# The last token chunk transposed by one DMA, into a tile-major layout

## The chip, the cores and the metric

One core of a Trainium2 chip. The metric is the device time of one execution, in microseconds (us). A profile is one execution taken by the hardware profiler; its times count from the start of its span. Engines: TensorE (PE, with weight loads apart as PEld), VectorE (DVE), ScalarE (ACT), GpSimd (POOL), and SyncE (SP), which here only issues DMAs. L12 is line 12 of the kernel.

## The reference

Tokens x are 2048 x 512, in bf16. They are normalised, and two branches are added to x: a filter in the frequency domain over both axes, and a gated MLP of width 1792.

```python
x = A_x                                   # (1, 2048, 512)
xn = _layernorm(x, axis=-1)
# A: rfft2 over tokens and features, times w_r + 1j * w_i (2048 x 257), irfft2
# B: h = gelu(xn @ w_gate) * (xn @ w_up);  h @ w_down
return x + _A_ref(xn, A_w_r, A_w_i) + _B_ref(xn, B_w_gate, B_w_up, B_w_down)
```

## The kernel before, in words

**Tiling.** The tokens are 16 tiles of 128 (j), and these are four chunks of 512 (m for the filter, b for the MLP). x stays in SBUF as `x_sb` with tokens on the partitions. Both branches contract over features, so both need the normalised tokens transposed: `xnT` (L251), features on 128 partitions, four groups of 128 features (dc), 2048 tokens in a row for each group, in fp16.

**How a chunk gets into xnT.** `ln_stat` and `ln_aggr` (L379 to L389) make mean and variance on DVE, and the reciprocal deviation on POOL. `ln_norm` (L391) writes one normalised tile into `xn`, a ring of four tiles, 128 x 2048 in all, which shares the buffer `cmx` with `ev1`. `trans` (L395) has TensorE transpose eight 128x128 blocks into a PSUM bank (L402), and then one copy puts the bank into `xnT`: DVE for feature groups 0 and 1 (L412), ACT for 2 and 3 (L414). A chunk takes two calls. Chunk 0 is done in part tile by tile by `trans1` (L1005 to L1014).

**Who reads xnT.** `butter` (L416) adds and subtracts feature halves on DVE: L422 and L423 over two feature groups of a chunk (1024 elements a partition each), L425 and L426 after them over 512. The results, the folds, are the stationary operands of `unit_D` (L430, matmuls L439 to L443), one call a tile, the first step of the filter's transform. From there `units_A` stores to DRAM (scr1, on SP), `load_tv` reads back (on SP), and `unit_B` (L571), `unit_C` and, near the end, `unit_E` and `unit_F` follow. `gate` and `up` (L859, L873) read xnT as the moving operand, 512 tokens at a time, in four matmuls over the feature groups (L868, L883); ACT makes the gelu (L871), DVE the product hT (L889). `product` (L743) is the down projection, done in seven products over sums (`sum_01`, L705; `sums_S`, L687; `sums_T`, L734) in place of eight. The sums are written over parts of xnT that are no longer read: `sum_01` over chunk 0's place, `sums_S` for the last chunk over that of chunks 0 to 2.

**What sets the order.** `_Prog.op` appends each operation to the list of its engine in program order, and derives the semaphore waits from keys read and written; each engine runs its list in order. The main loop (b, then the 14 feature groups fc) emits gate and up. After each of them `hook` runs the calls that were planned for that hook's number with `at(h, ...)`. Chunk 3's normalisation is planned at hooks 23 to 29, its two trans at 33 and 34, butter(3) at 35 and 36, unit_D(12) to (15) at 39 to 42, units_A(3) at 44, load_tv(3) at 47. On SP, the loads of filter weights `load_W` (L340) for slot 1 are planned at hooks 29 and 30, and load_tv(1) at 30, in this order. PSUM banks are chosen by `take` (L324), which keeps an estimate of when each bank comes free; each call moves the estimates of all later ones.

```python
            at(t, (trans, m, (0, 1), (0, 1, 2, 3)))
            at(t + 1, (trans, m, (2, 3), (0, 1, 2, 3), "act"))
            at(t + 2, (butter, m, 0))
            at(t + 3, (butter, m, 1))
```

Of the kernel before, what the change touches and what calls it, by code (L numbers as in the profile page):

```python
# [8 lines left out]
ALU = mybir.AluOpType  # L9
BF16 = mybir.dt.bfloat16  # L10
F16 = mybir.dt.float16
F32 = mybir.dt.float32  # L12

S = 2048
# [4 lines left out]
P = 128  # L19
NJ = 16  # L20
# [194 lines left out]
def bass_parallel_sum__spectral_gfnet__glu_gated_geglu__prompt_kernel(  # L215
# [27 lines left out]
    with ExitStack() as es:  # L243
        def sb(name, shape, dt):
            return es.enter_context(nc.sbuf_tensor(name, shape, dt))

        pr = _Prog(nc, es)
        op = pr.op

        x_sb = sb("x_sb", [P, NJ, D], BF16)  # L250
        xnT = sb("xnT", [P, 4, S], F16)  # L251
        arena = sb("arena", [P, 8192], F16)
        am = arena[:, 0:3072].rearrange("p (j c) -> p j c", j=NJ)
        fold = [arena[:, 4096 + 2048 * i:6144 + 2048 * i].rearrange("p (a c) -> p a c", a=4) for i in range(2)]
# [2 lines left out]
        wg_sb = sb("wg", [P, 4, FF], BF16)  # L257
        wu_sb = sb("wu", [P, 4, FF], BF16)
# [10 lines left out]
        ev1 = cmx[:, 0:1024].rearrange("p (a c) -> p a c", a=2)  # L269
        xn = cmx[:, 1024:3072].rearrange("p (a d) -> p a d", a=4)  # L270
# [23 lines left out]
        row = sb("row", [32, 64], BF16)  # L294
# [16 lines left out]
        def bank(i):  # L311
            return psum[:, i * 512:(i + 1) * 512]

        def bank_h(i):
            return psum_h[:, i * 1024:(i + 1) * 1024]
# [79 lines left out]
        def trans(m, dcs, jjs, eng="dve"):  # L395
            bk = take(1, 0.45, 1.2)
            def f(e):
                ins = None
                for a, dc in enumerate(dcs):
                    for c, jj in enumerate(jjs):  # L400
                        i = a * len(jjs) + c
                        ins = e.transpose(bank_h(bk)[:, i * P:(i + 1) * P], xn[:, jj, dc * P:(dc + 1) * P], ident[:])  # L402
                return ins
            op("pe", f, r=["ident"] + [("xn", jj) for jj in jjs], w=[("ps", bk)])
            w = len(jjs) * P
            c0 = m * 512 + jjs[0] * P
            n = len(dcs)
            dst = xnT[:, dcs[0]:dcs[0] + n, c0:c0 + w]
            src = bank_h(bk)[:, 0:n * w].rearrange("p (a c) -> p a c", a=n)
            ks = [("xnT", m, dc, jj) for dc in dcs for jj in jjs]  # L410
            if eng == "dve":
                op("dve", lambda e: e.tensor_copy(dst, src), r=[("ps", bk)], w=ks)  # L412
            else:
                op("act", lambda e: e.activation(dst, src, ACT.Copy), r=[("ps", bk)], w=ks)  # L414

        def butter(m, part):  # L416
            f = fold[m % 2]
            k = ("fold", m % 2)
            sl = slice(m * 512, (m + 1) * 512)
            xk = [("xnT", m, dc, jj) for dc in range(4) for jj in range(4)]  # L420
            if part == 0:
                op("dve", lambda e: e.tensor_tensor(ev1, xnT[:, 0:2, sl], xnT[:, 2:4, sl], ALU.add), r=xk, w=["ev1"])  # L422
                op("dve", lambda e: e.tensor_tensor(f[:, 2:4, :], xnT[:, 0:2, sl], xnT[:, 2:4, sl], ALU.subtract), r=xk, w=[k + (2,), k + (3,)])  # L423
            else:
                op("dve", lambda e: e.tensor_tensor(f[:, 0, :], ev1[:, 0, :], ev1[:, 1, :], ALU.add), r=["ev1"], w=[k + (0,)])  # L425
                op("dve", lambda e: e.tensor_tensor(f[:, 1, :], ev1[:, 0, :], ev1[:, 1, :], ALU.subtract), r=["ev1"], w=[k + (1,)])  # L426
# [225 lines left out]
               r=r + keys + [("x", j, 0), ("x", j, 1)], w=keys)  # L652

        eb7 = [early[:, 1792 * k:1792 * k + 1792].rearrange("p (f c) -> p f c", f=7) for k in range(4)]
        xb = xnT[:].rearrange("p d s -> p (d s)")
        cb = cmx[:]

        def ssum(b, k, f0, f1):
            if b == 2:
                return eb7[k][:, f0:f1, :]  # L660
            if k == 3:
                v = cb[:, 256 * f0:256 * f1]
            elif f1 <= 6:
                v = xb[:, 2048 * k + 256 * f0:2048 * k + 256 * f1]
            else:
                v = xb[:, 2048 * 3 + 256 * k:2048 * 3 + 256 * k + 256]
            return v.rearrange("p (f c) -> p f c", c=256)

        def s_keys(b, k, f0, f1):
# [45 lines left out]
        def s01(b, p, k, f0, f1):  # L715
            q = b == 0 and p == 1
            if k == 0 and b + p == 0:
                v = twh[:, 1024 + P * f0:1024 + P * f1]
            elif k == 0:
                v = arena[:, 7168 + P * f0:7168 + P * f1]  # L720
            else:
                assert f1 <= 4 or f0 >= 4
                o = P * (f0 % 4)
                if q and k in (1, 3):
                    v = fd[:, o:o + P * (f1 - f0)] if f0 >= 4 else dumm[:, o:o + P * (f1 - f0)]
                else:
                    row = 2 * (k == 2) + (f0 >= 4)
                    v = xb[:, 2048 * row + o:2048 * row + o + P * (f1 - f0)]
            return v.rearrange("p (f c) -> p f c", c=P)

        def sums_T(k):
# [127 lines left out]
        def gate(b, fc, jjs=(0, 1, 2, 3)):  # L859
            k = gun[0]  # L860
            n = len(jjs) * P
            c0 = b * 512 + jjs[0] * P
            bg = take(1, 0.0017 * n)

            def fn(e):
                ins = None
                for dc in range(4):
                    ins = e.matmul(bank(bg)[:, 0:n], wg_sb[:, dc, fc * P:(fc + 1) * P], xnT[:, dc, c0:c0 + n], start=(dc == 0), stop=(dc == 3))  # L868
                return ins
            op("pe", fn, r=[("wg", fc)] + [("xnT", b, dc, jj) for dc in range(4) for jj in jjs], w=[("ps", bg)])  # L870
            op("act", lambda e: e.activation(gl[k % 3][:, 0:n], bank(bg)[:, 0:n], ACT.Gelu_apprx_tanh), r=[("ps", bg)], w=[("gl", k % 3)])  # L871

        def up(b, fc, jjs=(0, 1, 2, 3), wait=False):  # L873
            k = gun[0]
            gun[0] += 1
            n = len(jjs) * P
            c0 = b * 512 + jjs[0] * P
            bu = take(1, 0.0017 * n, 2.2)

            def fn(e):  # L880
                ins = None
                for dc in range(4):
                    ins = e.matmul(bank(bu)[:, 0:n], wu_sb[:, dc, fc * P:(fc + 1) * P], xnT[:, dc, c0:c0 + n], start=(dc == 0), stop=(dc == 3))  # L883
                return ins
            op("pe", fn, r=[("wu", fc)] + [("xnT", b, dc, jj) for dc in range(4) for jj in jjs], w=[("ps", bu)])
            h0 = jjs[0] * P

            def mult():
                op("dve", lambda e: e.tensor_tensor(hT[b % 2][:, fc, h0:h0 + n], bank(bu)[:, 0:n], gl[k % 3][:, 0:n], ALU.mult),  # L889
                   r=[("ps", bu), ("gl", k % 3)], w=[("hT", b % 2, fc, jj) for jj in jjs])  # L890
            if wait:
                later.append(mult)
            else:
                mult()
# [28 lines left out]
        def at(h, *calls):  # L923
            plan.setdefault(int(h), []).extend(calls)
# [12 lines left out]
        for i in range(4):  # L937
            f0, f1 = (0, 4, 8, 11, 14)[i:i + 2]
# [12 lines left out]
        for m in range(1, 4):  # L951
            a = (5, 15, 23)[m - 1]
            t = (16, 25, 33)[m - 1]
            for i in range(4):
                at(a + i, (ln_stat, 4 * m + i))
            at(a + 3, (ln_aggr, 4 * m, 4))
            for i in range(4):
                at(a + 5 + i // 2, (ln_norm, 4 * m + i))
            at(t, (trans, m, (0, 1), (0, 1, 2, 3)))
            at(t + 1, (trans, m, (2, 3), (0, 1, 2, 3), "act"))  # L960
            at(t + 2, (butter, m, 0))
            at(t + 3, (butter, m, 1))
        at(3, (butter, 0, 0))
# [35 lines left out]
        def trans1(j, engs):  # L999
            for i, eng in enumerate(engs):  # L1000
                bk = take(1, 0.12, 1.0)
                def f(e, i=i, bk=bk):
                    ins = None
                    for a in range(2):
                        ins = e.transpose(bank_h(bk)[:, a * P:(a + 1) * P], xn[:, j, (2 * i + a) * P:(2 * i + a + 1) * P], ident[:])  # L1005
                    return ins
                op("pe", f, r=["ident", ("xn", j)], w=[("ps", bk)])
                dst = xnT[:, 2 * i:2 * i + 2, j * P:(j + 1) * P]
                src = bank_h(bk)[:, 0:256].rearrange("p (a c) -> p a c", a=2)
                ks = [("xnT", 0, 2 * i + a, j) for a in range(2)]  # L1010
                if eng == "dve":
                    op("dve", lambda e, dst=dst, src=src: e.tensor_copy(dst, src), r=[("ps", bk)], w=ks)
                else:
                    op("act", lambda e, dst=dst, src=src: e.activation(dst, src, ACT.Copy), r=[("ps", bk)], w=ks)  # L1014
# [108 lines left out]
```

## Time and profile before

| | |
|---|---|
| median of 13 runs | 183.08 us (182.71 to 184.56) |
| the profiled execution | 183.06 us, span 181.2 us |
| busy: PE, DVE, ACT, POOL | 175.1, 133.6, 95.7, 54.5 us |
| DMA | 26.84 MB, mean 148 GB/s |
| L402, transposes by TensorE (trans) | 56 of 219 ns |
| L412 / L414, copies of 128x1024 | 674 / 1017 ns |
| L422, L423 / L425, L426 | 681, 684 / 416, 417 ns |

The busy table gives each engine's share of the span. The chain of work that ended last is followed back from the last instruction; a piece of it is what the end had to wait for. Matmuls are pipelined: one of 512 columns has a record of about 0.38 us, but four of them take 0.86 us of the chain. In a time order, the number in brackets is the idle time of the engine before the instruction and who ended it. In the table of DMA issues, the last column is the time from issue to landing.

### The profile page before, as it was taken

To read this page: it belongs to the slowest core of one execution; us is meant where nothing else is said; L and a number is where in the kernel's file an instruction comes from. 1 tells how busy PE (TensorE), PEld (TensorE's weight loads), DVE (VectorE), ACT (ScalarE), POOL (GpSimd) and SP (SyncE) were. 2 spreads that over 40 slices of the span, in tenths; PEclk is the share of its full clock that TensorE was granted. 3 is DMA by queue.
4 is the path that set the end of the run, shared out by engine and by line. 5 is a ranking of instruction groups with operands and counts; after the bars stand their busy time and mean duration, and the time that the engine had idled before them with its cause. 6 is when DMAs were issued, how large, how long until landed. Compare 5 with 4: busy or idle time off the path is not lost.

```text
span 181.2 us, 3873 instructions
## 1 busy us (share of the span) xinstructions
PE 175.1 (97%) x1438; PEld 110.1 (61%) x1438; DVE 133.6 (74%) x333; ACT 95.7 (53%) x160; POOL 54.5 (30%) x107
## 2 busy tenths in 40 slices
PE   7699999999999999999999999999999999999992
PEld 2288745564646556556655556556666767666882
DVE  0776989999386695786875749797877777897552
ACT  2244556767686631475656655336858677632110
POOL 2210081816130406276580000001354625640000
PEclk9999999999999999999999999999999999999999
DMA  4999998476946363478763121393155755742104
GB/s 124 277 279 312 345 264 304 129 216 171 231 110 151 108 167 105 116 188 205 210 173 93 58 61 58 109 269 147 24 98 103 127 116 85 123 73 43 33 2 116
DMA packets 26739, 26.84 MB, mean 148 GB/s; under 512 B 2928, under 2 KB 23536, under 8 KB 26592
## 3 DMA queue, kind: packets, MB, share of 16 engines
q1 hardware_dynamic: 20640, 17.91, 36.1%
q0 software_dynamic: 4272, 7.24, 17.8%
q10 hardware_dynamic: 1808, 1.44, 3.2%
q8 instruction: 11, 0.18, 0.4%
q14 instruction: 8, 0.07, 0.1%
HBM read 18.19 MB, written 6.29 MB: 135 GB/s over the span
## 4 chain that ended last, share of the span: by engine, by line
PE 82%; DVE 11%; DMA 2%; issue 2%; POOL 1%; ACT 0%; DVEq 0%
PE ps L772 23%; PE ps L883 23%; PE ps L868 22%; DVE st L380 3%; DMA x_sb<-in_A_x_dram 2%; PE ps L596 2%; PE ps L624 2%; PE ps L826 2%; DVE hT L889 2%; PE ps L571 2%; PE ps L402 1%; DVE arena L734 1%; POOL rstd L388 1%; PE ps L471 1%; DVE cmx L392 1%
## 5 line engine op out<-in xcount | busy, mean ns | idle before, releaser
L868 PE MATMUL ps<-xnT,wg 128*128 128x512 f16 (+1 forms) x248 | 58.6, 359 | 0.5 <-ACT xnT L1014 0.5
L883 PE MATMUL ps<-xnT,wu 128*128 128x512 f16 (+1 forms) x248 | 58.6, 359 | 0.0
L889 DVE TENSOR_TENSOR hT<-ps,gl 128x512 bf16<-128x512 f32 (+1 forms) x62 | 39.2, 635 | 23.5 <-PE ps L883 17.7
L871 ACT ACTIVATE gl<-ps 128x512 bf16<-128x512 f32 (+1 forms) x62 | 34.5, 556 | 37.5 <-PE ps L868 37.0
L883 PEld LDWEIGHTS ps<-xnT,wu 128*128 128x128 bf16 x248 | 23.3, 98 | 19.2 <-issue 1.2
L868 PEld LDWEIGHTS ps<-xnT,wg 128*128 128x128 bf16 x248 | 23.2, 98 | 15.8 <-issue 1.4
L340 POOL DMA_DIRECT2D wring<-in_A_w_r_dram x32 | 18.5, 614 | 19.1 <-PE ps L772 9.8
L633 POOL COPY tv<-tv 1x128 bf16<-1x128 bf16 x16 | 5.4, 339 | 41.5 <-ACT tv L631 41.4
L772 PE MATMUL ps<-wd,hT 128*128 128x256 bf16 x112 | 14.4, 273 | 0.0
L852 POOL DMA_DIRECT2D x_sb<-tv x16 | 13.2, 866 | 3.4 <-DVE tv L845 2.4
L380 DVE BATCH_NORM_STATS2 st<-x_sb 128x6 f32<-128x512 bf16 x16 | 10.6, 681 | 3.7 <-DMA x_sb<-in_A_x_dram 3.7
L582 DVE TENSOR_TENSOR early<-early,wring 128x1024 bf16<-128x1024 f16 x16 | 10.4, 688 | 3.8 <-ACT early L577 3.8
L791 ACT ACTIVATE ps<-ps 128x256 f32<-128x256 f32 x16 | 5.9, 369 | 13.2 <-PE ps L772 13.1
L447 ACT ACTIVATE early<-ps 128x512 f16<-128x512 f32 x16 | 9.5, 596 | 5.7 <-PE ps L443 5.7
L772 PEld LDWEIGHTS ps<-wd,hT 128*128 128x128 bf16 x112 | 10.7, 98 | 2.5
L388 POOL TENSOR_TENSOR rstd<-vpe,mhalf 128x4 f32<-128x4 f32 (+2 forms) x6 | 5.0, 837 | 22.4 <-DVE vpe L387 22.4
L832 ACT ACTIVATE tv<-ps 128x512 bf16<-128x512 f32 x16 | 9.5, 595 | 3.6 <-PE ps L826 3.6
L772 PE MATMUL ps<-arena,xnT 128*128 128x256 f16 x91 | 11.4, 273 | 0.0
L631 ACT ACTIVATE tv<-ps 128x512 bf16<-128x512 f32 x16 | 9.5, 595 | 3.2 <-PE ps L624 3.2
L577 ACT ACTIVATE early<-ps 128x1024 f16<-128x1024 f32 x8 | 8.2, 1022 | 4.8 <-PE ps L571 4.8
L772 PEld LDWEIGHTS ps<-arena,xnT 128*128 128x128 f16 x91 | 8.6, 98 | 2.3 <-DVE tw L795 0.3
L651 DVE TENSOR_TENSOR x_sb<-ps,tw 128x256 bf16<-128x256 f32 x16 | 6.7, 421 | 2.9 <-PE ps L772 2.6
(118 smaller groups left out, 245.2 us busy)
## 6 DMA issues: line engine op xcount, KB each, us to landing
wring<-in_A_w_r_dram POOLq DMA_DIRECT2D x32, 64.2 KB, 3.2
wring<-in_A_w_i_dram SPq DMA_DIRECT2D x32, 64.2 KB, 3.3
tv<-scr SPq DMA_DIRECT2D x8, 256.0 KB, 4.0
scr<-early SPq DMA_DIRECT2D x8, 256.0 KB, 2.2
wring<-scr SPq DMA_DIRECT2D x4, 512.0 KB, 6.6
x_sb<-tv POOLq DMA_DIRECT2D x16, 128.0 KB, 2.7
scr<-early SPq DMA_DIRECT2D x15, 128.0 KB, 2.8
out_dram<-x_sb SPq DMA_DIRECT2D x28, 64.0 KB, 2.2
```

What stands on the lines that cost most here:

```text
L340: op(eng, lambda e: e.dma_start(dst, src), w=list(keys) + list(also), dma=True, after=[("pe", pr.cnt["pe"])])
L380: op("dve", lambda e: e.bn_stats(st[:, j, :], x_sb[:, j, :]), r=[("x", j, 0), ("x", j, 1)], w=[("st", j)])
L447: op("act", lambda e: e.activation(x4.rearrange("p (a c r) -> p a c r", a=2, r=4), bank(bk).rearrange("p (a r c) -> p a c r", a=2, r=4), A ...
L582: op("dve", lambda e, k=k: e.tensor_tensor(pp[i][k], xc[i], W[k][g % 4][:, :, :, 0:256], ALU.mult), r=[("xc", i)] + [key for c in range(2) ...
L631: op("act", lambda e: e.activation(z, bank(bk).rearrange("p (a c) -> p a c", a=4), ACT.Copy, scale=SC_E), r=[("ps", bk)], w=[zk] + (TVK if ...
L772: ins = e.matmul(o, st_(f), mv(f), start=(f == 0 and step in (0, 5)), stop=(f == 6), skip_group_check=True)
L832: op("act", lambda e: e.activation(o2, bank(bk), ACT.Copy), r=[("ps", bk)], w=[ok] + (TVK if j < 2 else []))
L852: op("pool", lambda e: e.dma_start(x_sb[:, j, :], ys, accum_op=ALU.add), r=[yk + (0,), yk + (1,), ("x", j, 0), ("x", j, 1)] + acc(j), w=ac ...
L868: ins = e.matmul(bank(bg)[:, 0:n], wg_sb[:, dc, fc * P:(fc + 1) * P], xnT[:, dc, c0:c0 + n], start=(dc == 0), stop=(dc == 3))
L871: op("act", lambda e: e.activation(gl[k % 3][:, 0:n], bank(bg)[:, 0:n], ACT.Gelu_apprx_tanh), r=[("ps", bg)], w=[("gl", k % 3)])
L883: ins = e.matmul(bank(bu)[:, 0:n], wu_sb[:, dc, fc * P:(fc + 1) * P], xnT[:, dc, c0:c0 + n], start=(dc == 0), stop=(dc == 3))
L889: op("dve", lambda e: e.tensor_tensor(hT[b % 2][:, fc, h0:h0 + n], bank(bu)[:, 0:n], gl[k % 3][:, 0:n], ALU.mult), r=[("ps", bu), ("gl", k ...
```

## The change

`xnT` becomes tile-major: for each tile of 128 tokens the four feature groups follow each other, 128 tokens each. The moving operand of gate and up is then four runs of 128 elements at a distance of 512, where it was one run of 512; butter reads the same blocks through a pattern of tile, group and token. `trans` and `trans1` put the transposed blocks into PSUM in the new order. The sums that are written over xnT are placed anew, over the same chunks as before.

For chunk 3 alone, both trans calls are left out. In their stead `trans_dma` is planned at hook 30: one DMA on SP's queue, which transposes the whole ring `xn` (128 x 2048 in fp16, 512 KB) into chunk 3's part of xnT, sixteen blocks of 128x128. It stands on SP behind the four W loads of slot 1 and ahead of the two loads of load_tv(1), and waits for DVE's last ln_norm. The first operation of butter(3) on DVE waits for the DMA. The order on the other engines stays, less the instructions that are gone; the PSUM banks after that point are partly others.

```diff
-        xnT = sb("xnT", [P, 4, S], F16)
+        xnT = sb("xnT", [P, NJ, 4, P], F16)
...
+        def trans_dma(m):
+            op("sp", lambda e: e.dma_start_transpose(xnT[:, 4 * m:4 * m + 4].rearrange("p j d c -> p (j d) c"), xn.rearrange("p a d -> p (a d)")),
+               r=[("xn", i) for i in range(4)], w=[("xnT", m, dc, jj) for dc in range(4) for jj in range(4)], dma=True)
+
...
-                op("dve", lambda e: e.tensor_tensor(ev1, xnT[:, 0:2, sl], xnT[:, 2:4, sl], ALU.add), r=xk, w=["ev1"])
-                op("dve", lambda e: e.tensor_tensor(f[:, 2:4, :], xnT[:, 0:2, sl], xnT[:, 2:4, sl], ALU.subtract), r=xk, w=[k + (2,), k + (3,)])
+                op("dve", lambda e: e.tensor_tensor(jac(ev1), xnT[:, js, 0:2, :], xnT[:, js, 2:4, :], ALU.add), r=xk, w=["ev1"])
+                op("dve", lambda e: e.tensor_tensor(jac(f[:, 2:4, :]), xnT[:, js, 0:2, :], xnT[:, js, 2:4, :], ALU.subtract), r=xk, w=[k + (2,), k + (3,)])
...
-                    ins = e.matmul(bank(bg)[:, 0:n], wg_sb[:, dc, fc * P:(fc + 1) * P], xnT[:, dc, c0:c0 + n], start=(dc == 0), stop=(dc == 3))
+                    ins = e.matmul(bank(bg)[:, 0:n], wg_sb[:, dc, fc * P:(fc + 1) * P], xnT[:, j0:j0 + len(jjs), dc, :], start=(dc == 0), stop=(dc == 3))
...
-            at(t, (trans, m, (0, 1), (0, 1, 2, 3)))
-            at(t + 1, (trans, m, (2, 3), (0, 1, 2, 3), "act"))
+            if m < 3:
+                at(t, (trans, m, (0, 1), (0, 1, 2, 3)))
+                at(t + 1, (trans, m, (2, 3), (0, 1, 2, 3), "act"))
+            else:
+                at(a + 7, (trans_dma, m))
```

More of the change, by code (lines that the diff above doesn't have):

```diff
@@ L400, in f @@
                     for c, jj in enumerate(jjs):
-                        i = a * len(jjs) + c
+                        i = c * len(dcs) + a
                         ins = e.transpose(bank_h(bk)[:, i * P:(i + 1) * P], xn[:, jj, dc * P:(dc + 1) * P], ident[:])
@@ L404, in trans @@
             op("pe", f, r=["ident"] + [("xn", jj) for jj in jjs], w=[("ps", bk)])
-            w = len(jjs) * P
-            c0 = m * 512 + jjs[0] * P
             n = len(dcs)
-            dst = xnT[:, dcs[0]:dcs[0] + n, c0:c0 + w]
-            src = bank_h(bk)[:, 0:n * w].rearrange("p (a c) -> p a c", a=n)
+            j0 = 4 * m + jjs[0]
+            dst = xnT[:, j0:j0 + len(jjs), dcs[0]:dcs[0] + n, :]
+            src = bank_h(bk)[:, 0:n * len(jjs) * P].rearrange("p (j a c) -> p j a c", a=n, c=P)
             ks = [("xnT", m, dc, jj) for dc in dcs for jj in jjs]
@@ L418, in butter @@
             k = ("fold", m % 2)
-            sl = slice(m * 512, (m + 1) * 512)
+            js = slice(4 * m, 4 * m + 4)
+            jac = lambda t: t.rearrange("p a (j c) -> p j a c", j=4)
             xk = [("xnT", m, dc, jj) for dc in range(4) for jj in range(4)]
             if part == 0:
-                op("dve", lambda e: e.tensor_tensor(ev1, xnT[:, 0:2, sl], xnT[:, 2:4, sl], ALU.add), r=xk, w=["ev1"])
-                op("dve", lambda e: e.tensor_tensor(f[:, 2:4, :], xnT[:, 0:2, sl], xnT[:, 2:4, sl], ALU.subtract), r=xk, w=[k + (2,), k + (3,)])
+                op("dve", lambda e: e.tensor_tensor(jac(ev1), xnT[:, js, 0:2, :], xnT[:, js, 2:4, :], ALU.add), r=xk, w=["ev1"])
+                op("dve", lambda e: e.tensor_tensor(jac(f[:, 2:4, :]), xnT[:, js, 0:2, :], xnT[:, js, 2:4, :], ALU.subtract), r=xk, w=[k + (2,), k + (3,)])
             else:
@@ L654, in bass_parallel_sum__spectral_gfnet__glu_gated_geglu__prompt_kernel @@
         eb7 = [early[:, 1792 * k:1792 * k + 1792].rearrange("p (f c) -> p f c", f=7) for k in range(4)]
-        xb = xnT[:].rearrange("p d s -> p (d s)")
+        xb = xnT[:].rearrange("p j d c -> p (j d c)")
         cb = cmx[:]
@@ L662, in ssum @@
                 v = cb[:, 256 * f0:256 * f1]
-            elif f1 <= 6:
+            else:
                 v = xb[:, 2048 * k + 256 * f0:2048 * k + 256 * f1]
-            else:
-                v = xb[:, 2048 * 3 + 256 * k:2048 * 3 + 256 * k + 256]
             return v.rearrange("p (f c) -> p f c", c=256)
@@ L727, in s01 @@
                     row = 2 * (k == 2) + (f0 >= 4)
-                    v = xb[:, 2048 * row + o:2048 * row + o + P * (f1 - f0)]
+                    v = xb[:, 512 * row + o:512 * row + o + P * (f1 - f0)]
             return v.rearrange("p (f c) -> p f c", c=P)
@@ L861, in gate @@
             n = len(jjs) * P
-            c0 = b * 512 + jjs[0] * P
+            j0 = 4 * b + jjs[0]
             bg = take(1, 0.0017 * n)
@@ L876, in up @@
             n = len(jjs) * P
-            c0 = b * 512 + jjs[0] * P
+            j0 = 4 * b + jjs[0]
             bu = take(1, 0.0017 * n, 2.2)
@@ L882, in fn @@
                 for dc in range(4):
-                    ins = e.matmul(bank(bu)[:, 0:n], wu_sb[:, dc, fc * P:(fc + 1) * P], xnT[:, dc, c0:c0 + n], start=(dc == 0), stop=(dc == 3))
+                    ins = e.matmul(bank(bu)[:, 0:n], wu_sb[:, dc, fc * P:(fc + 1) * P], xnT[:, j0:j0 + len(jjs), dc, :], start=(dc == 0), stop=(dc == 3))
                 return ins
@@ L958, in bass_parallel_sum__spectral_gfnet__glu_gated_geglu__prompt_kernel @@
                 at(a + 5 + i // 2, (ln_norm, 4 * m + i))
-            at(t, (trans, m, (0, 1), (0, 1, 2, 3)))
-            at(t + 1, (trans, m, (2, 3), (0, 1, 2, 3), "act"))
+            if m < 3:
+                at(t, (trans, m, (0, 1), (0, 1, 2, 3)))
+                at(t + 1, (trans, m, (2, 3), (0, 1, 2, 3), "act"))
+            else:
+                at(a + 7, (trans_dma, m))
             at(t + 2, (butter, m, 0))
@@ L1007, in trans1 @@
                 op("pe", f, r=["ident", ("xn", j)], w=[("ps", bk)])
-                dst = xnT[:, 2 * i:2 * i + 2, j * P:(j + 1) * P]
+                dst = xnT[:, j, 2 * i:2 * i + 2, :]
                 src = bank_h(bk)[:, 0:256].rearrange("p (a c) -> p a c", a=2)
```

## The prediction

> **What bounds the kernel now.** I read the busy table first, then the chain of work that ended last, and then, for the stretch in which the last chunk is transposed (45 to 55 us), the chain, the time order of DVE, that of SP's queue and the DMA issues. From the page:
>
> ```profile
> PE 175.1 (97%) x1438; PEld 110.1 (61%) x1438; DVE 133.6 (74%) x333; ACT 95.7 (53%) x160; POOL 54.5 (30%) x107
> ...
> PE 82%; DVE 11%; DMA 2%; issue 2%; POOL 1%; ACT 0%; DVEq 0%
> ```
>
> TensorE is busy for 97% of the span and is 82% of the chain. So work taken off TensorE is worth its time, unless what replaces it is late. The chain around the last chunk's transposes (start, length):
>
> ```profile
> 46.22 0.86 PE ps L883 x4
> 47.09 0.45 PE ps L402 x8
> ...
> 48.73 0.45 PE ps L402 x8
> ...
> 54.04 0.86 PE ps L883 x4
> 54.91 0.06 PE ps L439
> ```
>
> The reader is to see two pieces of 0.45 us, L402 x8: these sixteen transposes are on the chain, with matmuls packed before and behind them. At 54.91 comes L439, the first matmul of unit_D(12), which reads the folds that butter(3) makes from the last chunk. DVE in the same stretch:
>
> ```profile
> 47.12 0.69 DVE L889 TENSOR_TENSOR hT<-ps,gl 128x512 bf16<-128x512 f32 x1 [1.69 <-PE ps L883]
> 47.73 0.68 DVE L412 COPY xnT<-ps 128x1024 f16<-128x1024 f16 x1
> 50.40 0.69 DVE L889 TENSOR_TENSOR hT<-ps,gl 128x512 bf16<-128x512 f32 x1 [1.99 <-PE ps L883]
> 51.01 0.68 DVE L422 TENSOR_TENSOR cmx<-xnT 128x1024 f16<-128x1024 f16 x1
> ...
> 52.55 0.42 DVE L426 TENSOR_TENSOR arena<-cmx 128x512 f16<-128x512 f16 x1
> 52.88 0.62 DVE L705 TENSOR_TENSOR tw<-hT 128x896 f16<-128x896 bf16 x1
> ```
>
> The brackets (idle before, releaser) say that DVE waits for TensorE here, not the reverse; but from 50.40 on it has no gap. L422 to L426 is butter(3): 51.01 to 52.97, or 1.96 us. SP's queue, and the DMAs issued from 44 to 53 us (KB each, us to landing):
>
> ```profile
> 44.49 2.58 SPq L340 DMA_DIRECT2D wring<-in_A_w_i_dram  x4
> 47.23 1.16 SPq L337 DMA_DIRECT2D tv<-scr  x2
> ```
>
> ```profile
> tv<-scr SPq DMA_DIRECT2D x2, 256.0 KB, 4.7
> wring<-in_A_w_i_dram SPq DMA_DIRECT2D x6, 64.2 KB, 2.8
> ```
>
> The new DMA stands in SP's queue between these two groups. The pair of tv loads carries the same 512 KB from the same moment, so it is the nearest row for its landing.
>
> **What the Trainium skill says.** "DMA: Bandwidth & Descriptors", in "Latency and other measured facts", gives a DMA transpose 261 GB/s with a non-contiguous middle dimension and about 350 to 400 GB/s otherwise. "VectorE: DVE Perf Modes", in "The three transpose paths", gives 1309 ns for one 128x128 block by DMA and 390 ns by TensorE. The two disagree for our sixteen blocks: about 2.0 us or 20.9 us. The trace of before has no DMA transpose, so it supports neither; the second page's 390 ns for TensorE is not met (one L402 lasts 219 ns, and eight of them hold the chain for 0.45 us, 56 ns each). "SBUF — State Buffer", in the note on cachelines under the port swizzle, says that accesses within a 16-byte line run at full bandwidth; runs of 128 elements of 2 bytes are whole lines, so the new layout should be read at full speed. DVE's rows agree: L582 reads runs of 256 out of 258 elements and takes 685 ns for 1024, as dense L422 does (681).
>
> **The change part by part.** The sum stands against the profiled execution: 183.06 us, which is its span of 181.2 and 1.86 around it; the median of 13 runs is 183.08, so no correction is needed.
>
> Removed: sixteen transposes of TensorE, two chain pieces of 0.45 less rounding: -0.89 us on the chain. One DVE copy (L412, 0.68 us) goes from a stretch where DVE idles for 1.99 us behind it: worth nothing. One ACT copy (L414, 1.02 us at 49.26): the gelu and the unit_D copies behind it come a little earlier, but TensorE does not wait for them now: nothing. Nothing else gets shorter.
>
> Moved in layout: the moving operand of 400 gate and up matmuls (50 groups of four on each of L868 and L883, 512 wide) becomes four runs of 128, where it was one run of 512. No row of before has a moving operand in such runs. Lower bound zero: the same bytes, no gain possible. Upper bound, an estimate: one column lost at each of three breaks, 0.86 us / 4 / 512 = 0.42 ns, 400 x 3 x 0.42 = 0.5 us. I take zero, and keep 0.5. The eight butter operations L422 and L423 get a pattern of 4x2x128; L705 writes from runs of 128 out of 512 (896 elements in 620 ns, which is on the same line as 681 for 1024), so I take zero. Those of chunks 0 and 1 lie on the chain (DVE bounds 17 to 34 us), so 50 ns each there would cost 0.2 us. The copies out of PSUM keep their sizes: zero. The PSUM banks are picked anew after the two takes are gone; that can shift waits by some tenths either way.
>
> Added: one DMA on SP. Its inputs, four L392 results, are written by 44.74; SP reaches it after the four W issues, at 44.49 + 2.58 = 47.1. Bounds of its landing T: the fixed part is 1.8 us (the smallest transfer on SP's queue, the 4 KB z256 row of mini(3)); with 2.0 us at 261 GB/s, T = 50.9. The tv pair: first issue 47.23, the second about 0.56 later, landed 4.7 after that, 52.5; 5.3 us for 512 KB in two issues, with W loads of POOL beside it (in windows of 1 us the DMA engines are full from 48 to 50). One issue fewer: 4.7, so T = 51.8; the page's 261 GB/s against the 299 moved from 48 to 49 us adds 0.24. I take T = 52.0. Upper end: sixteen blocks in series, T = 47.1 + 1.8 + 20.9 = 69.8.
>
> Who waits: butter(3) on DVE, and behind it in DVE's order a sum_01, the hT products (which release PSUM banks and gl buffers) and T. With TensorE 0.89 earlier, the hT product before butter ends at about 50.1, so DVE idles from then until T. TensorE itself first misses the fold: unit_D(12) had to load weights by 54.64 (matmul at 54.74), now 0.89 earlier, 53.75; less 1.96 for butter and some 0.05 of signalling: **T up to 51.75 is free, and each us later costs a us**. The next waits have more room: the first up behind unit_D(12), at 57.52 in the chain, so 56.6, needs the bank of the hT product that DVE ends about 3.1 after T (butter 1.96, a sum 0.55, the product 0.6): T up to 53.5. The SP issues behind the DMA (tv of chunk 1, W slot 2, scr stores) have slack: the first reader of tv, L571, runs at 74.14.
>
> Sum: 183.06 - 0.89 + (52.0 - 51.75 = 0.25) = 182.42.
>
> **The rivals.**
> The wash: T from 52.1 to 53.2. The mechanism is the same, the stall eats the gain; for it speaks that the tv pair landed at 52.5. T = 52.6 gives 183.06 - 0.89 + 0.85 = 183.0.
> Late landing, the side on which it ends slower: the crossbar does not reach plain rate, and butter(3) holds DVE and then unit_D(12) holds TensorE. It decides from T = 52.64 on, where the gain is spent, i.e. a DMA longer than 5.5 us from issue, and can be measured from 53.2 on. Against it speaks the page's 261 GB/s, for it the other page's 1309 ns per block, or 25 GB/s. Their geometric mean is 81 GB/s: 6.5 us, T = 55.4, stall 3.65: 185.8. I let this case reach T = 57.0, 187.4.
> Blocks in series: T = 69.8, stall 18.05: 200.2. The same wait at its far end; the DVE backlog would then bind as well.
> That the transposes do not vanish is excluded by the diff: the branch for m = 3 issues no trans.
>
> **How the numbers follow.** A measurement of this kernel tells about 0.3%, 0.55 us, from no change. Faster (T up to 52.1): 0.36, likeliest single case, 182.4, own range 181.9 to 182.5; 181.9 is the full -0.89 with 0.3 for luckier banks. Wash: 0.20. Late landing: 0.27. Series: 0.17. For slower stand the last two, 0.44. The range of 8 in 10 leaves out the series: 181.9 to 187.4; the layout's possible 0.5 us lies inside it.
>
> **What would show it.** Right: no L402 after 41 us; a transpose issued on SP near 47.1 and landed by 52.0; butter(3)'s first operation at T, after some 1.9 us of idle DVE; unit_D(12)'s first matmul at about 54.1; gate and up pieces still 0.86. Wrong: DVE idle for more than 2.5 us ahead of butter(3) with the DMA as releaser, and TensorE idle ahead of unit_D(12) (late landing); gate and up pieces longer than 0.86, or the butter operations above 0.69 (layout); a new idle piece of TensorE behind an hT product (banks).

## The result, and the profile after

| | before | after |
|---|---|---|
| median | 183.28 us (182.71 to 185.04, 48 runs) | 185.62 us (184.03 to 187.83, 11 runs) |
| profiled execution, span | 183.06, 181.2 | 185.62, 183.8 |
| ratio | | 1.0112, interval 1.0082 to 1.0142 |

The changed kernel is slower by about 1.1%, where 182.4 was forecast. Every ratio in this document compares undisturbed runs only, while medians and ranges take in all runs.

The page of after, the same two lines as shown of before:

```profile
PE 175.7 (96%) x1422; PEld 110.1 (60%) x1422; DVE 133.3 (73%) x332; ACT 94.8 (52%) x159; POOL 54.3 (30%) x107
...
PE 77%; DVE 12%; DMA 5%; issue 2%; POOL 1%; ACT 1%; DVEq 0%
```

Sixteen TensorE instructions are gone (1438 to 1422), but TensorE's share of the chain has fallen from 82% to 77%, and DMA's has gone from 2% to 5%. A wait has been put where work was. The chain of after shows it (start, length):

```profile
47.81 0.88 PE ps L885 x4
...
48.70 5.89 DMA xnT<-cmx
...
54.62 0.69 DVE cmx L426
...
56.25 0.34 DVE arena L430
56.59 0.04 issue
56.64 0.23 PE ps L443
```

The chain leaves TensorE for the DMA, passes through butter(3) on DVE (L426 to L430 here), and comes back at unit_D(12)'s first matmul (L443; L439 before). DVE and TensorE in the order of time, with the idle time ahead of the instruction in brackets:

```profile
51.10 0.69 DVE L891 TENSOR_TENSOR hT<-ps,gl 128x512 bf16<-128x512 f32 x1 [1.70 <-PE ps L885]
54.62 0.69 DVE L426 TENSOR_TENSOR cmx<-xnT 128x1024 f16<-128x1024 f16 x1 [2.83 <-DMA xnT<-cmx]
```

```profile
56.64 0.23 PE L443 MATMUL ps<-fd,arena 128*128 128x128 f16 x1 [1.04 <-DVE arena L430]
```

DVE stands still for 2.83 us with the DMA as releaser, then TensorE for 1.04 with butter as releaser. SP's queue, and the DMA issues from 44 to 56 us:

```profile
46.06 2.60 SPq L340 DMA_DIRECT2D wring<-in_A_w_i_dram  x4
48.70 1.78 SPq L416 DMA_TRANSPOSE xnT<-cmx  x1
50.65 1.18 SPq L337 DMA_DIRECT2D tv<-scr  x2
```

```profile
tv<-scr SPq DMA_DIRECT2D x2, 256.0 KB, 7.0
wring<-in_A_w_r_dram POOLq DMA_DIRECT2D x7, 64.2 KB, 6.4
...
xnT<-cmx SPq DMA_TRANSPOSE x1, 5.9
```

The DMA took 5.9 us from issue, not 4.9, and the two tv loads behind it 7.0 in place of 4.7.

Where the 2.56 us of span went can be told by lining up the 62 hT products of DVE, counted from 0, in both traces (start in after less start in before):

| up to | shift | step |
|---|---|---|
| product 6, 17 us | +1.59 | the start of the kernel |
| product 23, 51 us | +0.70 | -0.89, the transposes that left the chain |
| product 28, 68 us | +1.91 | +1.21, the late DMA |
| product 39, 104 us | +2.55 | +0.64, one wait at 100 us |
| the end | +2.55 | nothing more |

The first step comes before the new DMA is even issued. In the chain from 0 to 22 us, the pieces of gate and up (four matmuls of a tile each) last twice as long as the usual 0.44:

```profile
8.96 0.87 PE ps L870 x4
9.83 0.85 PE ps L885 x4
...
12.39 0.58 PE ps L870 x4
12.96 0.44 PE ps L885 x4
```

The granted clock of TensorE was 0.57 from 9 to 13 us, where it was 1.00 in before. The same stretch in before and then in after (length, busy PE, PEld, DVE, ACT, POOL; then the granted clock, the DMA share and GB/s):

```profile
9.00:13.00 4.00, 4.00 (x38) 3.59 (x37) 2.99 (x10) 1.54 (x4) 0.70 (x1) 1.00 1.07 270
9.00:13.00 4.00, 4.00 (x22) 2.94 (x23) 2.15 (x8) 0.77 (x2) 0.71 (x1) 0.57 1.07 261
```

A low clock of this kind, from here on a dip, comes in some runs of before as well (see the section on why). The last step of the table is a gelu that the first matmuls of unit_C (L600) wait for, in the chain from 98 to 103 us:

```profile
98.69 0.88 PE ps L870 x4
99.56 0.02 issue
99.59 0.61 ACT gl L873
100.19 0.14 issue
100.33 0.63 PE ps L600 x16
```

### The profile page after: what moved, and what is told of

Its sections match the earlier page's. It is cut to its first block, busy times and chain, and to the rows that moved or that the text cites. A ratio compares the mean times of both kernels' runs of the same rounds, so it can differ in the third digit from the quotient of the medians.

```text
span 183.8 us, 3842 instructions
## 1 busy us (share of the span) xinstructions
PE 175.7 (96%) x1422; PEld 110.1 (60%) x1422; DVE 133.3 (73%) x332; ACT 94.8 (52%) x159; POOL 54.3 (30%) x107
## 2 busy tenths in 40 slices
DMA packets 28819, 27.36 MB, mean 149 GB/s; under 512 B 5008, under 2 KB 25616, under 8 KB 28672
## 4 chain that ended last, share of the span: by engine, by line
PE 77%; DVE 12%; DMA 5%; issue 2%; POOL 1%; ACT 1%; DVEq 0%
PE ps L774 23%; PE ps L885 22%; PE ps L870 21%; DVE st L380 3%; DMA xnT<-cmx 3%; PE ps L600 2%; DMA x_sb<-in_A_x_dram 2%; PE ps L828 2%; PE ps L628 2%; DVE hT L891 2%; PE ps L575 1%; DVE arena L736 1%; DVE cmx L426 1%; POOL rstd L388 1%; DVE cmx L392 1%
## 5 line engine op out<-in xcount | busy, mean ns | idle before, releaser
L870 PE MATMUL ps<-xnT,wg 128*128 128x512 f16 (+1 forms) x248 | 59.5, 363 | 0.5 <-ACT xnT L1019 0.5
L885 PE MATMUL ps<-xnT,wu 128*128 128x512 f16 (+1 forms) x248 | 59.5, 363 | 0.0
L870 PEld LDWEIGHTS ps<-xnT,wg 128*128 128x128 bf16 x248 | 23.7, 99 | 16.2 <-issue 1.6
```

## The experiments

Theory at the outset: within the kernel the mechanism of the prediction holds, with a landing that is later than I took it. Rivals: the layout costs something; the DMA disturbs others; and for the start, that it belongs to the change. The runs come in four sets, each on one chip of its own with its own runs of before: e1 to e4, e5 to e8, e9 to e12, e13 to e16. Every ratio is against the runs of before in the same set. "Shift" is that of the hT products against the profiled before.

**e1_layout.** The layout alone: chunk 3 is transposed by TensorE again.

```diff
-            if m < 3:
+            if m < 4:
```

> The tile-major layout alone, all chunks transposed by TensorE. Late-landing theory: the layout costs nothing, so the time of before within 0.3% (183.1 to 183.6), gate and up pieces 0.86 us, butter operations 0.68 us. Rival (the four short runs of the moving operand, or the new patterns on DVE, cost time): 1 us or more above before.

183.23, ratio 1.0003 (0.9972 to 1.0034); the shift stays at -0.18 from product 5 to the end. The layout is free, as the prediction took it.

**e2_banks.** After, with two empty calls of `take` in the place of the two trans, so that PSUM banks are as before.

```diff
             else:
                 at(a + 7, (trans_dma, m))
+                at(t, (take, 1, 0.45, 1.2))
+                at(t + 1, (take, 1, 0.45, 1.2))
```

> The changed kernel with the planner's two takes kept, so that the PSUM banks are those of before. Late-landing theory with a share for the banks: 0.6 us less than the changed kernel, ratio to before 1.008, the wait of unit_C on a gelu at about 100 us gone, the stall ahead of unit_D(12) unchanged at 1.2 us or more. If banks are no part of it: ratio 1.011 as the changed kernel.

187.82, ratio 1.0148 (1.010 to 1.0196): not the 1.008 that was expected, but for other reasons. Its start lost 2.35 us and its DMA took 6.8 us. The step at 100 us is gone: the shift is +3.56 at product 28 and +3.56 at the end, as it is level from product 28 on in e4 and e9 below, which keep the banks too. In its chain unit_C follows unit_B with no gelu between them:

```profile
105.43 0.34 PE ps L575 x8
105.78 0.44 PE ps L600 x16
```

So the 0.64 us are the banks that were picked anew.

**e3_unused.** Before, with the same 512 KB transposing DMA at the same place on SP, but into a spare tile that nobody reads; TensorE still transposes.

```diff
+        spare = sb("spare", [P, NJ, P], F16)
...
+        def trans_dma(m):
+            op("sp", lambda e: e.dma_start_transpose(spare[:], xn.rearrange("p a d -> p (a d)")),
+               r=[("xn", i) for i in range(4)], w=["spare"], dma=True)
...
+            if m == 3:
+                at(a + 7, (trans_dma, m))
```

> The kernel before with the same 512 KB transposing DMA at the same place in SP's queue, into a spare tile that nobody reads; TensorE transposes as before. Late-landing theory: the wait is the cost, so within 0.3% of before; the DMA lands 5.5 to 7 us after its issue. Rival (the DMA's traffic and SP's longer issue slow the loads around it): 1 us or more above before.

187.43, ratio 1.0172 (1.0125 to 1.0219). The shift is +3.96 by 17 us and +3.96 at the end: the DMA, issued at 51.05 and landed 6.8 us later, cost nothing, and all was lost before it was issued. The waits up to 22 us and the chain name what was late there, ACT's loads of w_gate (us in total, times, longest):

```profile
PE ps L873 <- DMA wg<-in_B_w_gate_dram: 2.4, 1, 2.4
```

```profile
2.65 11.36 DMA wg<-in_B_w_gate_dram
...
14.05 1.03 PE ps L873 x4
15.08 0.85 PE ps L888 x4
15.94 0.85 PE ps L873 x4
```

After the wait the clock is low again (pieces of 0.85 for 0.44). This left a new question, what makes w_gate late.

**e4_first.** e2, with SP's four W loads of slot 1 (i > 3) moved two hooks later, behind the DMA. POOL's four stay in place.

```diff
-                at(h0 + i // 2, t)
+                at(h0 + i // 2 + 2 * (s == 1 and i > 3), t)
```

> As the kernel with the banks kept, and the four W loads of slot 1 on SP's queue placed behind the transpose, so that it is issued at about 44.8 on the clock of before instead of 47.1. Late-landing theory: with 5.9 us it lands at 50.7, ahead of the free limit of 51.75, so the full gain of the transposes shows: 182.2 to 182.5, ratio 0.995 to 0.997. Rival (contention or another cost than the wait): ratio 1.005 or more.

184.92, ratio 1.0088 (1.005 to 1.0125). The profiled run lost 5.87 us at the start, then the shift falls to +4.97 at product 23 and is +4.98 at the end: the 0.89 us are gained and nothing is given back. The DMA landed 4.9 us after issue.

**e5_tiny, e6_plain, e8_quiet.** Three unread DMAs in before, which measure the disputed cost. e5: one block of 128x128, 32 KB, at SP's place. e6: the 512 KB copied within SBUF, without a transpose, at the same place. e8: the 512 KB transpose at 60 us, where the DMA engines are idle (their share in before is 0.01 and less from 60 to 63 us). e3's diff, with these lines in it for e5, e6 and e8 in turn (in e8 the DMA also waits for what TensorE has been given up to that hook):

```diff
-            op("sp", lambda e: e.dma_start_transpose(spare[:], xn.rearrange("p a d -> p (a d)")),
-               r=[("xn", i) for i in range(4)], w=["spare"], dma=True)
+            op("sp", lambda e: e.dma_start_transpose(spare[:], xn[:, 0, 0:P]), r=[("xn", 0)], w=["spare"], dma=True)
```

```diff
-            op("sp", lambda e: e.dma_start_transpose(spare[:], xn.rearrange("p a d -> p (a d)")),
+            op("sp", lambda e: e.dma_start(spare[:].rearrange("p j c -> p (j c)"), xn.rearrange("p a d -> p (a d)")),
```

```diff
-                at(a + 7, (trans_dma, m))
+                at(44, (trans_dma, m))
```

> The kernel before with a transposing DMA of one 128x128 block (32 KB) at the same place in SP's queue, into a spare tile that nobody reads. Start theory (a program that holds a crossbar transpose starts worse: the first wg pieces on ACT's queue land later in the first 17 us, long before the transpose is issued): 1 to 2% above before, with the loss complete by 20 us. Rival (the 512 KB of traffic are what costs): within 0.3% of before.

> The kernel before with a plain DMA of the same 512 KB, from SBUF to SBUF, at the same place, into a spare tile that nobody reads. Start theory: no transpose in the program, so within 0.3% of before. Rival (traffic): 1 to 2% above before. It lands about 4 us after its issue, against 5 to 7 for the transpose.

> The kernel before with the unread 512 KB transpose issued at about 60.3 us on its clock, where the DMA engines are idle. Its landing tells the transfer by itself: 5 us or more if the crossbar sets it, 4 us if what stood in the queues did. Start theory: 1 to 2% above before, all of it in the first 20 us. Rival (traffic beside the W loads): within 0.3% of before.

Times: 183.24, ratio 1.0006 (0.9985 to 1.0026); 183.07, 0.9992 (0.9965 to 1.0019); 183.08, 0.9998 (0.9977 to 1.0018). None costs anything that can be measured, so on this chip a transposing DMA on SP's queue did not spoil the start, against the start theory. The landings tell more. The DMA issues of e5, e6 and e8, in this order:

```profile
spare<-cmx SPq DMA_TRANSPOSE x1, 3.7
```

```profile
spare<-cmx SPq DMA_DIRECT2D x1, 512.0 KB, 6.4
```

```profile
spare<-cmx SPq DMA_TRANSPOSE x1, 3.8
```

By itself the 512 KB transpose takes 3.8 us, hardly more than one block among the traffic (3.7). At SP's place a plain copy of the same bytes takes 6.4, no less than the transpose (5.9 to 7.0 in seven profiles). So it isn't the transposing that is slow; it is what else is under way there. Which of the transfers there delays it was not tested one by one.

**e7_act.** Before, with an unread 32 KB transpose on ACT's queue instead of SP's.

```diff
+            op("act", lambda e: e.dma_start_transpose(spare[:], xn[:, 0, 0:P]), r=[("xn", 0)], w=["spare"], dma=True)
```

> As the kernel with the 32 KB transpose, but issued on ACT's queue. If a transpose leaves its own queue's rings ahead for the start of the next execution, ACT's loads come first and the start is as in before, within 0.3% (plus up to 1 us for ACT's time in the issue). If any transpose in the program spoils the start: 1 to 2% above before.

Inconclusive on its question: 185.56 in the middle of 182.62 to 189.19 (22 runs). Eight runs lie from 182.6 to 183.1, the others from 184.2 to 189.2; the profiled one (span 181.0) is of the eight, with a landing of 4.4 us. What it showed is that a loss of the size of e3's comes and goes from run to run of one kernel: 12 of its 22 runs took 185.4 us or more, and none of the other 125 runs on this chip did.

**e9 to e12: who goes first.** In e2, e3 and e4 the first packets on SP's queue start at 2.1 us and those on ACT's at 2.2 to 2.8; in before, e1, e5 to e8 and in after's profile it is ACT's at 2.1 and SP's at 2.5 to 2.7. SP's second issue shows it as well, first in before, then in e3:

```profile
1.39 0.81 SPq L337 DMA_DIRECT2D wu<-in_B_w_up_dram  x1
```

```profile
1.39 0.56 SPq L338 DMA_DIRECT2D wu<-in_B_w_up_dram  x1
```

Both engines issue their first load at 0.74 us. Either can be held back to 0.87 by a wait for POOL's small memset. e10 holds back ACT in before; e9 holds back SP in e4, e11 in after, e12 in e3.

```diff
-        def load_x(j0, n, b, eng):
+        def load_x(j0, n, b, eng, r=()):
...
-            load_x(0, 2, b, eng)
+            load_x(0, 2, b, eng, ["mhalf"] if eng == "act" else ())
```

> The kernel before, with one thing changed: ACT's first load (x) waits for the small memset of mhalf on POOL (0.74 to 0.84 us in every trace so far), so that SP's queue gets its loads going first. No transposing DMA in it. Theory A (the loss in the first 20 us of the slow kernels is the order in which SP's and ACT's queues get their first loads through: w_gate comes late, TensorE waits and its clock falls): reproduces it, 184.5 to 188, ratio 1.008 to 1.025, runs scattered by 2 us or more, SP's second load issue at 0.56 us instead of 0.81. Theory B (the loss is tied to the transposing DMA or to chance, not to the order): same as before, within 0.3%.

> The kernel e4_first (transposing DMA ahead of four of SP's W loads, banks as before), and SP's first load waits for the memset of mhalf, so that ACT's queue goes first. Theory A: the start is as before, and the 0.89 us of the transposes that left the chain are seen whole: 182.2 to 182.5, ratio 0.994 to 0.997, runs within 0.5 us of each other but for those with the usual clock dip. Theory B: as e4_first, ratio 1.005 to 1.0125, scattered.

> The changed kernel, with SP's first load waiting for the memset of mhalf (ACT's queue first). Theory A: start as before; what is left is -0.89 of transposes, +1.2 of the late DMA and +0.6 of the banks at 99 to 102 us, so +0.9 to +1.0: 184.0, ratio 1.003 to 1.007. Theory B: as the changed kernel, ratio 1.008 to 1.014.

> The kernel before, with the 512 KB transposing DMA into a spare tile that nobody reads, at SP's place (e3_unused), and SP's first load waiting for the memset of mhalf. Theory A: same as before, ratio 0.998 to 1.002 (the DMA by itself cost nothing at 47 to 55 us in e3_unused). Theory B: as e3_unused, ratio 1.0125 to 1.022.

| | median (range), us | ratio |
|---|---|---|
| e10, SP first | 186.81 (185.41 to 189.21) | 1.0156 (1.0094 to 1.0218) |
| e9, ACT first | 183.21 (181.65 to 184.01) | 0.9967 (0.9938 to 0.9996) |
| e11, ACT first | 184.89 (183.59 to 186.89) | 1.0052 (1.0023 to 1.0082) |
| e12, ACT first | 182.99 (182.62 to 184.88) | 0.9973 (0.9935 to 1.001) |

The ratios of e9, e10 and e11 lie where theory A had them; that of e12 is just below, with 1 in its interval. The medians of e9 and e11 are 0.7 to 0.9 us above what A gave, and their runs further apart than it said. A hold of 0.13 us on ACT costs about 3 us, with no transposing DMA in the kernel. The waits up to 22 us in e10, and its stretch from 13 to 17 us (the columns as above; the granted clock is 0.56):

```profile
PE ps L868 <- DMA wg<-in_B_w_gate_dram: 4.8, 2, 4.3
```

```profile
13.00:17.00 4.00, 1.42 (x7) 1.02 (x8) 0.32 (x2) 0.35 (x1) 0.00 (x0) 0.56 1.12 320
```

TensorE is busy for 1.42 us of 4, and then at half its clock. e9 is also the one kernel here that is faster than before by its interval, by 0.3%. Its shift is +1.20 at product 22 (the low clock at the start, as in after's profile), +0.30 at product 23 and +0.30 at the end, so the 0.89 stay. The ratio alone would not prove the gain, since that of e12, where nothing was taken off TensorE, is nearly as low. Runs with and without the dip (mean clock below or above 0.993) tell them apart:

| median, us (runs) | no dip | dip |
|---|---|---|
| before, this set | 182.96 (33) | 184.68 (18) |
| e9 | 182.35 (13) | 183.62 (9) |
| e12 | 182.89 (12) | 184.62 (2) |

Like against like, e9 gains 0.6 and 1.1 us, and e12, with the same hold on SP, less than 0.1. DVE in e9, where butter(3) now follows the product without idling, and the DMA in the table of issues from 44 to 57 us:

```profile
50.70 0.69 DVE L891 TENSOR_TENSOR hT<-ps,gl 128x512 bf16<-128x512 f32 x1 [1.69 <-PE ps L885]
51.31 0.68 DVE L426 TENSOR_TENSOR cmx<-xnT 128x1024 f16<-128x1024 f16 x1
```

```profile
xnT<-cmx SPq DMA_TRANSPOSE x1, 4.8
```

**e13 to e16: is the order the change's doing?** After (e13), e3 (e14) and e5 (e15) once more, unchanged, on one chip; and before with SP held back, nothing else (e16).

> The changed kernel as it is, on the chip of this call. If the order of the first loads belongs to the program, its runs and its trace are as measured before: ratio 1.008 to 1.014, scattered over 3 us or more. If it belongs to the chip or to the moment, they may come out either as that or as the kernel with the forced order: 1.003 to 1.007, nothing above 187.

> The unread 512 KB transposing DMA in the kernel before, as it was in e3_unused. Order belongs to the program: SP's queue goes first again (second SP issue at 0.56 us), ratio 1.0125 to 1.022. Order belongs to the chip or the moment: same as before, 0.998 to 1.002, or a mixture of the two.

> The unread 32 KB transposing DMA, as in e5_tiny, which differs from e14_unused_again by the size of one DMA only. Order belongs to the program: same as before (0.998 to 1.002) beside an e14_unused_again that is slow. Order belongs to the chip: both slow or both as before.

> The kernel before with nothing but SP's first load waiting for the memset of mhalf (ACT's queue first). If the kernel before already has ACT's queue first in its runs, nothing changes: ratio 0.998 to 1.002, and the gain of e9_first_order is that of the transposes alone. If some of its runs have the other order, it gains by up to 0.3%.

| | median (range), us | ratio |
|---|---|---|
| e13, after | 185.02 (184.42 to 188.41) | 1.0097 (1.0064 to 1.0129) |
| e14, 512 KB unread | 183.26 (182.70 to 184.80) | 1.0012 (0.9989 to 1.0036) |
| e15, 32 KB unread | 183.01 (182.64 to 187.87) | 0.9998 (0.9976 to 1.002) |
| e16, ACT first | 183.00 (182.54 to 184.67) | 0.999 (0.9959 to 1.0021) |

e14 is the kernel that was 1.7% slower on the first chip; here it is as before. e15 is as before too, but its profiled run came out at 187.87, with SP first (its second issue took 0.56 us) and w_gate late (the waits up to 22 us):

```profile
PE ps L872 <- DMA wg<-in_B_w_gate_dram: 3.3, 1, 3.3
```

One of the 51 runs of before in this set took 187.18; it has no trace. So the order isn't fixed by the program: the profiles of both kernels have one order on their first chip and the other here (e3 SP, e14 ACT; e5 ACT, e15 SP), and times of 185.4 us and more came in all of e3's runs and in none of e14's. e16 gains nothing that can be measured, so the gain of e9 is not the hold on SP, as e12 shows too.

e13's profile has a clean start and shows the change alone: shift -0.14 at product 22, -1.03 at 23, +0.75 at 28, +1.38 at the end. That is -0.89, +1.78 and +0.63, so +1.5 us by the change itself in this run, which is the fastest of its six. Counted in the same way, without the start, the profiles of after and e11 have +0.96 and +2.0; the three differ in the stall alone (1.21, 1.78 and 2.26). The runs without the dip fit: they have medians of 185.30 (after, 6 runs), 184.99 (e13, 5) and 184.60 (e11, 17), where the 136 such runs of before in the four sets have 183.03. So the change by itself costs 1.0 to 2.0 us in the profiles, and 1.6 to 2.3 in these medians. DVE and the DMA's issue in e13:

```profile
46.98 1.93 SPq L416 DMA_TRANSPOSE xnT<-cmx  x1
```

```profile
53.45 0.69 DVE L426 TENSOR_TENSOR cmx<-xnT 128x1024 f16<-128x1024 f16 x1 [3.39 <-DMA xnT<-cmx]
```

## Why the prediction was wrong, step by step

The step that failed is the landing of the DMA, put at T = 52.0 and measured at 53.0 to 54.0. The PSUM banks, which stand in the sum at nothing, added 0.64 us, and the profiled execution lost 1.59 more at its start, for which the sum had no term.

**Transposes off the chain, -0.89: right.** All six traces with the DMA in use show 0.89 or 0.90 between products 22 and 23.

**Layout at nothing: right.** e1: 1.0003; in after the first two butter operations last 680 and 682 ns (681 and 684 before).

**SP reaches the DMA at 47.1: right.** e13: 46.98, with a start that is 0.14 earlier.

**Landing, "One issue fewer: 4.7, so T = 51.8 [...] I take T = 52.0": failed.** This is the step that turned the sign: with the stall as measured, -0.89 + 1.21 is +0.32 in after, and -0.89 + 1.78 is +0.89 in e13. The table puts each landing on the clock of before (issue, plus time to landing, less the shift at product 22), and beside it the stall that "T up to 51.75 is free, and each us later costs a us" gives:

| | issue | to landing | T | stall by the rule | measured |
|---|---|---|---|---|---|
| after | 48.70 | 5.9 | 53.0 | 1.26 | 1.21 |
| e13 | 46.98 | 6.5 | 53.6 | 1.87 | 1.78 |
| e2 | 49.46 | 6.8 | 53.9 | 2.16 | 2.10 |
| e11 | 48.73 | 6.9 | 54.0 | 2.28 | 2.26 |
| e9 | 45.96 | 4.8 | 49.6 | 0 | 0.00 |
| e4 | 50.63 | 4.9 | 49.7 | 0 | 0.00 |

The rule holds within 0.1 us in all four late landings, and the two early ones cost nothing. The signs that the prediction named for a late landing came too: DVE idle for more than 2.5 us behind the DMA (2.83), then TensorE idle ahead of unit_D(12) (1.04).

What was wrong was T alone, by 1.0 to 2.0 us, and so was the row that I took it from: the pair of tv loads of before landed in 4.7 us at that place, but no 512 KB that the experiments put ahead of it did, transposing or not (e6). The Trainium skill's figure was sound: "DMA: Bandwidth & Descriptors", in "Latency and other measured facts", has 261 GB/s with a non-contiguous middle dimension, which with the 1.8 us of fixed cost from before's trace makes an estimate of 3.8 us, and e8 measured 3.8 (the 350 to 400 GB/s that the page has otherwise would make 3.1 to 3.3). It is the time on idle DMA engines. To that, the traffic at this place adds 2 to 3 us, where I had added some tenths. The 1309 ns for a block, in "VectorE: DVE Perf Modes", "The three transpose paths", from which I made a chance of 0.17 for sixteen blocks in series and a part of the late landing, does not add up by blocks: sixteen took 3.8 us in e8, one took 3.7 in e5. Taking four W loads of SP from ahead of the DMA (e4, e9) brought it to 4.9 and 4.8 and its issue forward by 2.3 us (e9: 45.96 less 1.20 is 44.8, for 47.1), and the stall was gone. The edit took the loads away and moved the issue forward at once, so which of the two shortened the landing is not told apart.

So the outcome lies between the wash (T up to 53.2), where after's profile falls with 53.0, and the late landing (55.4). Who waits for whom was as in both of them. The reason that the late landing gave, a crossbar below plain rate, was not it: a plain copy is as late at that place (6.4 us), and the transpose takes 3.8 on idle engines. That 185.62 comes so near to the late landing's 185.8 is luck: by its landing alone after's profile would stand at 183.38 (183.06 - 0.89 + 1.21), and the banks and the start make up the rest.

**Banks, "some tenths either way": right in kind, not in the sum.** It was +0.64, one wait of unit_C at 100 us (after, e11, e13), and 0 with banks as before (e2, e4, e9).

**The start: missing from the sum.** The prediction had no term for the first 20 us, since nothing in the diff touches them. In after's profile they are +1.59. With it and the two sizes the sum closes for this one execution: 182.42 + (1.21 - 0.25) + 0.64 + 1.59 = 185.61, for 185.62 measured. It isn't shown to be the change's own: 44 of the 180 runs of before in the four sets have a mean TensorE clock below 0.993, as after's profile has (0.989), and take 184.1 us or more (median 184.6, where the other 136 have 183.03); e14's profile, without the change, shows the low clock too (1.01 us lost); and w_gate came late in kernels with SP first whether the transposing DMA was read, unread, tiny or absent. It isn't ruled out either. On the chip of e1 to e4 all six runs of e3 take 185.4 us or more, though nobody reads its DMA, where the 17 runs of before and e1 reach 184.5 at most; and e7 has such runs where its neighbours have none. With ACT held first by the edit (e11), after is slower by 0.5%; as it is, on another chip (e13), by 1.0%. The runs without the dip, 1.6 and 2.0 us above before, differ less.

**Open.** What decides which queue goes first when neither is held: e3's profile had SP first on one chip and ACT first on another (e14), from the same program. Whether a transposing DMA later in the program makes SP first likelier on some chips is not settled by these runs. What sets off the low clock in after's profile, where w_gate was in time, is open too. And so is why e11's runs spread over 3.3 us with ACT first. The dip accounts for a part (its runs without it spread over 2.3 us); its landings may differ from run to run (5.9 to 7.0 are seen in profiles, worth 1.1 us), but no profile of its fastest runs was taken.

## What to carry to other kernels

Price a DMA by itself and by its place. The time on idle engines says what the operation can do, not when it lands, and here even a row from the same stretch and queue (the tv loads, 4.7 us) was 1.2 to 2.3 us too short. Compare the landing with the latest time that is free, with room for such a miss, and put the DMA ahead of loads that can wait (e9). An edit that takes operations out of a planned schedule moves the choices behind it too (here PSUM banks, +0.64 us), and empty calls keep them in place. A small ratio needs its loss located in time first: here a part of it lay before anything that the change touches.

## What the runs showed of the hardware that was not expected

- Two queues whose first loads are issued at the same 0.74 us: a delay of 0.13 us for one decides which is served first, and cost about 3 us (e10), by late weights and then a TensorE clock of 0.56 for some microseconds.
- A transposing DMA holds its issuing queue longer than a plain one: 1.25 us for 32 KB and 1.7 to 3.4 us for 512 KB on SP, against 0.60 for the plain 512 KB of e6.
- The 512 KB transpose adds 2080 packets (26739 to 28819 in after), and the count of those under 512 B rises by as many (2928 to 5008); it still lands in 3.8 us on idle engines.
